# Holding back the fourth to seventh load at the start of a fused memory-attention and FFN kernel

## The chip, the cores and the metric

The kernel runs on one core of one Trainium2 chip. The metric is the device time of one execution in microseconds, lower is better; the time of the kernel before is the median of three runs.

## The reference

An attention over a small memory is followed by a bilinear feed-forward network without activation. Per batch (8) and head (8), with 576 positions, head width 64 and 32 memory slots:

```
a    = softmax(phi, over the 576 positions)          # [576, 32]
k_m  = a^T k ;  v_m = a^T v                          # [32, 64] each
attn = softmax(q k_m^T / 8, over the 32 slots)       # [576, 32]
x    = attn v_m                                      # heads side by side: [4608, 512]
out  = (((x w1) * (x w2)) w3) w_out                  # w1, w2: 512 x 1024, w3: 1024 x 1024, w_out: 1024 x 512
```

q, k, v and phi are float32; the four weights are float64 in memory, so w3 is 8 MB and each of the other three 4 MB.

## The kernel before, in words

**Algebra.** Because nothing stands between `w3` and `w_out`, the kernel forms their product W once (L386 to L403, `product` and `keep`), and it folds the attention's values into `w1` and `w2` per batch (`memory_weights`, L288). What is left per batch is `ab_unit` (the two products and their elementwise product, L437) and `out_part` (the product with W, L464). Both run as three matmuls each on values split into a high and a low part.

**Start.** The tasks of the list `tasks` (L321 to L325) are pieces of the weights: 18 of them go through five rotating buffers called `raw` (`BUFS = 5`, L328), the first four 512 KB each, the rest 1024 KB each. In order they are: `w3` and `w_out` alternately (rows 0 to 127, 128 to 255, then 256 rows at a time), the other column half of `w3`, then `w1` and `w2`. `fetch(i)` (L334) issues the load of task i; `convert(i)` (L350) turns its float64 words into float32 with two instructions of ScalarE (L378, L379) and three of VectorE (L377, L381, L382). Converting frees the buffer of task i, and `next_tile` (L407) then fetches task i + 5 into it. So before the loop over `START` (L415) five loads are issued at once, and the sixth follows the first conversion, the seventh the second, and so on. The first matmuls, `product(0, k)` at L392, need the converted `w3` and `w_out` rows of step k: W00 the first two tasks, W01 the next two, W02 and W03 the fifth and the sixth.

**Order.** All loads and stores of the kernel go through one queue, that of SyncE (SP). The orders of SP and of TensorE are as written in the program (lists `START`, `FIRST`, `SECOND`, `STEADY`, L22 to L37; L574). The orders of ScalarE and VectorE are laid out when the kernel is built, by simulated times. In `START`, C is `next_tile`, Wrk is `product(r, k)`, Krk is `keep`, N one step of `memory_weights`; phi0, kv0 and q0 are the loads of batch 0 (`load_phi` L121, `load_kv` L126, `load_q` L140); top, exp, norm, turn, mem, blocks, sc, se, sn, pr are the steps of the attention. The SP order at the start is: tasks 0 to 4, 5, 6, 7, 8, phi0, 9, 10, 11, kv0 (four transfers), 12, q0, 13 and on.

Of the kernel before, what the change touches and what calls it, by code (L numbers as in the profile page):

```python
# [8 lines left out]
F32 = mybir.dt.float32  # L9
# [31 lines left out]
def memory_attention__then__bilinear_ffn_kernel(  # L41
# [21 lines left out]
    nc = tc.nc  # L63
    P = 128
    B, NG, _, S = qT.shape
    D = 64
    M = 32
    NT = 2
# [8 lines left out]
    const = ctx.enter_context(tc.tile_pool(name="const", bufs=1))  # L77
# [40 lines left out]

    loaded = {}

    def load_phi(b):  # L121
        t = att.tile([P, NT, S], F32, name="ph", tag="ph")
        nc.sync.dma_start(out=t, in_=phiT[b].rearrange("t p s -> p t s"))
        loaded["ph", b] = t

    def load_kv(b):  # L126
        t = []
        for i in range(0, 4, 2):
            x = att.tile([P, 2, 8 * 2 * D], F32, name=f"kv{i}", tag=f"kv{i}")
            src = kv[b, i * P : (i + 2) * P].rearrange("(c p) h x -> p c (h x)", c=2)  # L130
            nc.sync.dma_start(out=x, in_=src)
            t += [x[:, j] for j in range(2)]

        x = att.tile([P, NG * 2 * D], F32, name="kv4", tag="kv4")
        for j in range(NT):
            src = kv[b, 4 * P :, j * NG : (j + 1) * NG].rearrange("s h x -> s (h x)")
            nc.sync.dma_start(out=x[j * D : (j + 1) * D], in_=src)
        loaded["kv", b] = [*t, x]

    def load_q(b):  # L140
        t = att.tile([P, NG, S], F32, name="q", tag="q")
        nc.sync.dma_start(out=t, in_=qT[b].rearrange("g p s -> p g s"))
        loaded["q", b] = t

    LOADS = {"phi": load_phi, "kv": load_kv, "q": load_q}

    def load(what, b):
# [178 lines left out]
    FIRST_LATE = 18  # L326
# [7 lines left out]
    def fetch(i):  # L334
        if i >= len(tasks):
            return
        kind, _, n, src = tasks[i]
        if i < FIRST_LATE:
            raw = init.tile([P, CW * 2], I32, name="raw", bufs=BUFS)
        else:  # L340

            name = ("kv0", "kv2", "q")[(i - FIRST_LATE) % 3]
            shape = [P, NG, S] if name == "q" else [P, 2, 8 * 2 * D]
            raw = att.tile(shape, F32, name=name, tag=name).bitcast(I32)
            raw = raw.rearrange("p a b -> p (a b)")
        words = n * src.shape[2] // 2
        raws[i] = raw[:, : 2 * words].rearrange("p (k x) -> p k x", k=n)
        nc.sync.dma_start(out=raws[i], in_=src)

# [57 lines left out]
    def next_tile():  # L407
        i = next(todo)
        convert(i)
        fetch(i + BUFS if i + BUFS < FIRST_LATE + 3 else i + 3 if i >= FIRST_LATE else len(tasks))  # L410

    with tc.tile_pool(name="init", bufs=1) as init:
        steps = [attention(b) for b in range(B)]
        m0 = memory_weights(0)
        for i in range(BUFS):  # L415
            fetch(i)
        for what in START:
            if what == "C":
                next_tile()
            elif what[0] == "W":  # L420
                product(int(what[1]), int(what[2]))
            elif what[0] == "K":
                keep(int(what[1]), int(what[2]))
            elif what == "N":
                m0.pop(0)()
            elif what[:-1] in LOADS:
                load(what, 0)
            else:
                steps[0][what]()
# [148 lines left out]
```

## Time and profile before

| | |
|---|---|
| median of three runs | 551.29 us (550.37 to 552.06) |
| the profiled execution | 550.54 us, of which the span from the first to the last instruction is 548.7 us |
| TensorE clock granted | 0.999 of the full one over the span |
| DMA, whole span | 64.05 MB, mean 117 GB/s |
| loads and stores | one queue, 24,944 packets |

The profile is of one execution. Times in its views count from the first instruction. PE is TensorE's matmuls, PEld its weight loads, DVE VectorE, ACT ScalarE, SP SyncE; SPq is an instruction with which SP issues a transfer. What stands behind an arrow in brackets ended the engine's idle time. The landing of a load is when its last byte is known to have arrived; the view of transfers gives the time from issue to landing.

### The profile page before, as it was taken

Reading aid. Unit: us, or ns where it says so; the run is one execution under the profiler, and the core shown is the slowest. Engines: PE = TensorE matmul, PEld = TensorE weight load, DVE = VectorE, ACT = ScalarE, POOL = GpSimd, SP = SyncE. Lnnn points to the kernel's source line nnn. Section 1 sums busy time; section 2 is a strip of 40 time slices with the busy share of each in tenths; the row PEclk is TensorE's granted clock in tenths of the full one; section 3 lists DMA queues with packets and bytes.
Section 4 is the critical chain, followed back from the end, with each engine's and each line's share of the span. In section 5 each row is a group of like instructions: output and inputs, shape, how many; then the busy total and the mean of one; then the engine's idle time right before and its main releaser. Section 6 shows DMA issues by size and latency. Waiting matters only on the chain.

```text
span 548.7 us, 9731 instructions
## 1 busy us (share of the span) xinstructions
PE 531.0 (97%) x4024; PEld 427.6 (78%) x4024; DVE 313.4 (57%) x600; ACT 249.9 (46%) x494; POOL 0.7 (0%) x6
## 2 busy tenths in 40 slices
PE   4899999999999999999999999999999999999997
PEld 1344357976998689968996899869986899689985
DVE  4877999557367715593458425673567045915400
ACT  5886966524554325452544335443544044514310
POOL 0000000000000000000000000000000000000000
PEclk9999999999999999999999999999999999999999
DMA  8999828036334510082007210351012100010011
GB/s 295 410 355 391 305 77 270 33 111 231 113 143 168 174 39 21 1 278 82 20 1 280 81 39 1 151 173 56 2 58 69 39 20 2 21 44 14 1 38 57
DMA packets 24987, 64.05 MB, mean 117 GB/s; under 512 B 1776, under 2 KB 2032, under 8 KB 24944
## 3 DMA queue, kind: packets, MB, share of 16 engines
q1 hardware_dynamic: 24944, 63.45, 32.6%
q8 instruction: 31, 0.51, 0.4%
q14 instruction: 12, 0.10, 0.1%
HBM read 54.00 MB, written 9.44 MB: 116 GB/s over the span
## 4 chain that ended last, share of the span: by engine, by line
PE 89%; DVE 7%; DMA 2%; issue 1%; ACT 1%; SPq 0%; DVEq 0%; ACTq 0%
PE o L472 37%; PE b L449 18%; PE a L449 18%; PE a L298 2%; PE a L392 2%; PE b L392 2%; DMA raw<-in_w3T 2%; DVE w L382 2%; PE o L199 2%; PE x L298 2%; PE x L184 1%; PE b L298 1%; PE x L199 1%; PE x L239 1%; DVE w L381 1%
## 5 line engine op out<-in xcount | busy, mean ns | idle before, releaser
L472 PE MATMUL o<-Wh,gh 128*128 128x512 f32 x288 | 115.4, 401 | 0.0
L472 PE MATMUL o<-Wl,gh 128*128 128x512 f32 x288 | 112.8, 391 | 0.0
L472 PE MATMUL o<-Wh,gl 128*128 128x512 f32 x288 | 112.5, 391 | 0.0
L460 DVE TENSOR_TENSOR gr<-b,a_sb 128x288 f32<-128x288 f32 x128 | 58.6, 458 | 85.9 <-PE b L449 82.0
L115 ACT CAST gh<-gr 128x288 fp32r<-128x288 f32 x128 | 55.4, 433 | 100.3 <-DVE gr L460 100.3
L116 DVE TENSOR_TENSOR gl<-gr,gh 128x288 fp32r<-128x288 f32 x128 | 58.6, 458 | 58.9 <-ACT gh L115 58.5
L449 PE MATMUL b<-ah,mh 128*128 128x288 f32 x256 | 76.0, 297 | 1.8 <-DVE gr L460 1.2
L449 PE MATMUL a<-ah,mh 128*128 128x288 f32 x256 | 77.2, 301 | 0.0
L449 PE MATMUL a<-al,mh 128*128 128x288 f32 x256 | 75.6, 295 | 0.1
L449 PE MATMUL b<-al,mh 128*128 128x288 f32 x256 | 75.5, 295 | 0.0
L449 PE MATMUL a<-ah,ml 128*128 128x288 f32 x256 | 75.3, 294 | 0.0
L449 PE MATMUL b<-ah,ml 128*128 128x288 f32 x256 | 75.3, 294 | 0.0
L472 PEld LDWEIGHTS o<-Wh,gh 128*128 128x128 f32 x288 | 54.1, 188 | 22.6 <-issue 11.9
L490 ACT COPY osb<-o 128x512 f32<-128x512 f32 x31 | 18.2, 586 | 100.1 <-PE o L472 87.4
L472 PEld LDWEIGHTS o<-Wl,gh 128*128 128x128 f32 x288 | 54.1, 188 | 12.4
L472 PEld LDWEIGHTS o<-Wh,gl 128*128 128x128 f32 x288 | 54.1, 188 | 10.9
L458 ACT COPY a_sb<-a 128x288 f32<-128x288 f32 x128 | 50.3, 395 | 3.5 <-PE a L449 3.1
L449 PEld LDWEIGHTS a<-ah,mh 128*128 128x128 f32 x256 | 48.0, 187 | 3.0 <-issue 1.0
L449 PEld LDWEIGHTS b<-ah,mh 128*128 128x128 f32 x256 | 48.0, 187 | 2.5 <-DVE gr L460 1.7
L449 PEld LDWEIGHTS a<-al,mh 128*128 128x128 f32 x256 | 48.1, 188 | 0.7 <-DVE al L116 0.3
L449 PEld LDWEIGHTS b<-ah,ml 128*128 128x128 f32 x256 | 48.2, 188 | 0.0
L449 PEld LDWEIGHTS a<-ah,ml 128*128 128x128 f32 x256 | 48.2, 188 | 0.0
(97 smaller groups left out, 650.8 us busy)
## 6 DMA issues: line engine op xcount, KB each, us to landing
kv<-in_kv SPq DMA_DIRECT2D x16, 1024.0 KB, 7.4
q<-in_qT SPq DMA_DIRECT2D x8, 1152.0 KB, 10.5
out<-osb SPq DMA_DIRECT2D x31, 256.0 KB, 2.0
raw<-in_w3T SPq DMA_DIRECT2D x7, 1024.0 KB, 11.8
ph<-in_phiT SPq DMA_DIRECT2D x8, 576.0 KB, 3.9
raw<-in_w SPq DMA_DIRECT2D x4, 1024.0 KB, 17.6
raw<-in_w_out SPq DMA_DIRECT2D x3, 1024.0 KB, 10.4
kv<-in_w SPq DMA_DIRECT2D x3, 1024.0 KB, 14.5
```

The costliest lines, as they stand in the source:

```text
L115: nc.scalar.copy(out=hi, in_=src)
L116: nc.vector.tensor_tensor(out=lo, in0=src, in1=hi.bitcast(F32), op=ALU.subtract)
L184: nc.tensor.transpose(ps[:, c, t], v["ph"][:, t, at : at + P], ident)
L199: nc.tensor.matmul(ps[t][h * M : (h + 1) * M, : 2 * D], lhsT=v["a"][:, i, t, h * M : (h + 1) * M], rhs=kvt[i][:, (4 * t + h) * 2 * D : (4 ...
L298: nc.tensor.matmul(ps[t][g * M : (g + 1) * M], lhsT=vm[b % 2][d, g], rhs=w12_sb[q][d, :, g], start=True, stop=True,)
L382: nc.vector.tensor_tensor(out=y, in0=y, in1=u, op=ALU.add)
L392: nc.tensor.matmul(pw[r][i], lhsT=x[:, i * P : (i + 1) * P], rhs=wos[k // half][:, k % half], start=k == 0, stop=k == NF - 1,)
L449: nc.tensor.matmul(p, lhsT=x[:, t, w, fc : fc + P], rhs=y[:, n, t * HALF : (t + 1) * HALF], start=i == 0, stop=i == len(todo) - 1,)
L458: nc.scalar.copy(out=a_sb, in_=ps[0])
L460: nc.vector.tensor_tensor(out=gr, in0=ps[1], in1=a_sb, op=ALU.mult)
L472: nc.tensor.matmul(v["p"], lhsT=x[f][:, at : at + P], rhs=y[f // half][:, f % half], start=f == 0 and k == 0, stop=f == NF - 1 and k == 2,)
L490: nc.scalar.copy(out=osb, in_=v["p"])
```

## The change

A one-row tile `gate` is added, and a helper `one_by_one`, called just ahead of the load of each `raw` tile and of batch 0's phi, kv and q. It counts the loads. Ahead of the load numbers 3, 4, 5 and 6 (counted from 0; the fourth to the seventh) it issues, in the same SP queue, a transfer of four bytes from the first element of an earlier load's tile into `gate`: number 3 behind number 0, 4 behind 1, 5 behind 3, 6 behind 4. Because that transfer reads what the earlier load writes, SP waits for that load's landing before it issues the four bytes; the load behind them is issued next and doesn't wait for the four bytes to land. Ahead of all other loads nothing is added.

```
+    BEHIND = {3: 0, 4: 1, 5: 3, 6: 4}
+    flights = []
+    gate = const.tile([1, 64], F32, name="gate")
+
+    def one_by_one(dst, words):
+        n = len(flights)
+        if n in BEHIND:
+            nc.sync.dma_start(out=gate[:, n : n + 1], in_=flights[BEHIND[n]][0])
+        flights.append([dst, words, False])
...
     def load_phi(b):
         t = att.tile([P, NT, S], F32, name="ph", tag="ph")
+        if b == 0:
+            one_by_one(t[:1, 0, :1], P * NT * S)
         nc.sync.dma_start(out=t, in_=phiT[b].rearrange("t p s -> p t s"))
...
         words = n * src.shape[2] // 2
+        if i < FIRST_LATE:
+            one_by_one(raw[:1, :1].bitcast(F32), P * 2 * words)
         raws[i] = raw[:, : 2 * words].rearrange("p (k x) -> p k x", k=n)
         nc.sync.dma_start(out=raws[i], in_=src)
```

The two calls left out, in `load_kv` and `load_q`, have the same form; none of the calls there or in `load_phi` issues anything, since those loads' numbers are not in `BEHIND`.

## Rows read from the trace of the kernel before

**Rows 1.** Stages of the span (view of windows): start and end, length, busy time and count of instructions of PE, PEld, DVE, ACT and POOL, granted clock, DMA share, GB/s.

```profile
0.00:20.00 20.00, 9.45 (x17) 4.04 (x18) 11.65 (x19) 13.11 (x15) 0.70 (x6) 1.00 0.90 332
20.00:49.00 29.00, 28.21 (x164) 13.36 (x162) 22.37 (x32) 20.62 (x25) 0.00 (x0) 1.00 1.03 379
49.00:87.00 38.00, 35.56 (x159) 18.20 (x158) 37.65 (x57) 29.62 (x34) 0.00 (x0) 1.00 0.59 214
87.00:548.70 461.70, 457.77 (x3687) 392.04 (x3687) 241.75 (x494) 186.56 (x421) 0.00 (x0) 1.00 0.24 83
```

**Rows 2.** The chain of waits that ended last, its start in order of time: start, length, what.

```profile
2.11 0.43 SPq L348
2.55 0.04 issue
2.59 10.64 DMA raw<-in_w3T
13.23 0.02 issue
13.26 1.17 ACT w L378
14.43 1.26 ACT u L379
15.69 0.02 issue
15.71 1.23 DVE w L382
...
18.30 1.24 DVE wo L382
19.54 0.04 issue
19.58 1.12 PE a L392 x2
...
40.58 0.86 PE b L392 x2
41.44 1.89 PE x L199 x64
```

**Rows 3.** Timeline of SP's issues: start, length of the issue, what.

```profile
0.73 0.39 SPq L348 DMA_DIRECT2D raw<-in_w3T  x1
1.18 0.42 SPq L348 DMA_DIRECT2D raw<-in_w_out  x1
1.64 0.43 SPq L348 DMA_DIRECT2D raw<-in_w3T  x1
2.11 0.43 SPq L348 DMA_DIRECT2D raw<-in_w_out  x1
2.59 0.47 SPq L348 DMA_DIRECT2D raw<-in_w3T  x1
5.36 0.37 SPq L348 DMA_DIRECT2D raw<-in_w_out  x1
7.36 0.37 SPq L348 DMA_DIRECT2D raw<-in_w3T  x1
10.68 0.37 SPq L348 DMA_DIRECT2D raw<-in_w_out  x1
12.08 0.37 SPq L348 DMA_DIRECT2D raw<-in_w3T  x1
12.50 0.46 SPq L123 DMA_DIRECT2D ph<-in_phiT  x1
...
85.82 0.89 SPq L131 DMA_DIRECT2D kv<-in_kv  x2
86.76 1.17 SPq L137 DMA_DIRECT2D kv<-in_kv  x2
87.97 0.59 SPq L142 DMA_DIRECT2D q<-in_qT  x1
```

**Rows 4.** View of transfers, asked for one issue at a time, for the first to the eighth load in that order, then the last of kv0's four (issued at 23.87 us): KB, and us from issue to landing.

```profile
raw<-in_w3T SPq DMA_DIRECT2D x1, 512.0 KB, 3.2
raw<-in_w_out SPq DMA_DIRECT2D x1, 512.0 KB, 4.8
raw<-in_w3T SPq DMA_DIRECT2D x1, 512.0 KB, 7.6
raw<-in_w_out SPq DMA_DIRECT2D x1, 512.0 KB, 8.6
raw<-in_w3T SPq DMA_DIRECT2D x1, 1024.0 KB, 10.6
raw<-in_w_out SPq DMA_DIRECT2D x1, 1024.0 KB, 10.4
raw<-in_w3T SPq DMA_DIRECT2D x1, 1024.0 KB, 11.0
raw<-in_w_out SPq DMA_DIRECT2D x1, 1024.0 KB, 10.2
...
kv<-in_kv SPq DMA_DIRECT2D x1, 128.0 KB, 16.6
```

**Rows 5.** Windows around the first loads, and around a later burst of issues (the last two rows); columns as in rows 1.

```profile
1.50:4.50 3.00, 0.00 (x0) 0.00 (x0) 0.46 (x1) 1.02 (x2) 0.00 (x0) 1.00 0.85 322
4.50:9.50 5.00, 1.38 (x2) 0.84 (x3) 2.83 (x6) 2.37 (x5) 0.00 (x0) 1.00 0.92 261
9.50:13.00 3.50, 3.50 (x6) 1.39 (x5) 2.75 (x6) 2.50 (x4) 0.00 (x0) 1.00 1.03 424
13.00:20.00 7.00, 4.56 (x11) 1.82 (x10) 5.61 (x7) 6.45 (x6) 0.00 (x0) 1.00 1.03 413
20.00:30.00 10.00, 10.00 (x25) 4.38 (x24) 9.03 (x14) 8.39 (x11) 0.00 (x0) 1.00 1.03 407
...
88.00:90.00 2.00, 2.00 (x24) 1.00 (x23) 1.84 (x7) 1.81 (x6) 0.00 (x0) 1.00 1.00 408
90.00:92.50 2.50, 2.50 (x21) 2.50 (x20) 2.47 (x5) 1.76 (x4) 0.00 (x0) 1.00 1.02 408
```

**Rows 6.** The shortest landings of the trace by median (page, DMA issues): stores of the result.

```profile
out<-osb SPq DMA_DIRECT2D x31, 256.0 KB, 2.0
```

More of the change, by code (lines that the diff above doesn't have):

```diff
@@ L130, in load_kv @@
             src = kv[b, i * P : (i + 2) * P].rearrange("(c p) h x -> p c (h x)", c=2)
+            if b == 0:
+                one_by_one(x[:1, 0, :1], P * 16 * 2 * D)
             nc.sync.dma_start(out=x, in_=src)
@@ L141, in load_q @@
         t = att.tile([P, NG, S], F32, name="q", tag="q")
+        if b == 0:
+            one_by_one(t[:1, 0, :1], P * NG * S)
         nc.sync.dma_start(out=t, in_=qT[b].rearrange("g p s -> p g s"))
```

## The prediction, made before the changed kernel ran

> **What bounds the kernel now.** I read the stages first [rows 1]. From 87 us to the end TensorE is busy 457.77 of 461.70 us at a granted clock of 1.00; the change touches nothing there, so that part only moves as a block. From 49 to 87 us VectorE is busy 37.65 of 38.00 us, again a block. From 20 to 49 us TensorE is busy 28.21 of 29.00 us. Only the first 20 us hold idle time: TensorE works 9.45 us of them. Next the chain of waits [rows 2]: it runs through SP's issues, then one load, the fifth (issued at 2.59 us, landed 10.64 us later at 13.23), then ScalarE and VectorE converting that load and the sixth, and reaches TensorE at 19.58 us, from where TensorE goes on to the attention step at 41.44 us. So what the change can be worth is how much earlier or later the fifth and sixth load land. Adding issue and landing time [rows 3, 4], the loads land at 3.9, 6.0, 9.2, 10.7, 13.2, 15.8, 18.4 and 20.9 us: in the order of issue, and from the fifth on one every 2.6 us, which is the queue at full rate, 407 to 424 GB/s [rows 5]. Between 4.5 and 9.5 us the rate was 261 GB/s although the DMA engines were busy for a 0.92 share [rows 5]: that slump is the one thing a different order of issue could cure.
>
> **The change part by part.**
>
> *The four small issues.* An issue takes SP 0.37 to 0.47 us [rows 3], so four take about 1.7 us. SP has nothing else to do at those times except the loads behind, so they count only through those.
>
> *The delays of issue.* The fourth load (2.11 us now) waits for the first landing: 3.9, plus 0.45 for the small issue, so about 4.4. The fifth (2.59) waits for the second: about 6.5. The sixth (5.36) waits for the fourth: about 11.2. The seventh (7.36) waits for the fifth: about 13.7. Queued behind it on SP are the eighth (10.68), the ninth (12.08) and phi (12.50), which go out at about 14.1, 14.6 and 15.1.
>
> *Does a landing move for it?* The first load took 3.2 us for 512 KB [rows 4]; at 413 GB/s its bytes take 524/413 = 1.27 us, so 1.95 us is what a load pays besides its bytes. From a landing to the landing that the released load could reach on an idle queue it is therefore 0.45 + 1.95 = 2.4 us plus its own bytes. What covers this are the loads still queued: the second and third behind the first, the third and fourth behind the second, the fifth behind the fourth, the sixth behind the fifth. Each time that is 1024 KB, 1049/413 = 2.54 us. The cover is enough by 0.14 us per gate, and by more in the slump. The eighth load must start to flow when the seventh's bytes end, just before 18.4 us; issued at 14.1, it has 1.95 us to spare twice over. I take 0.1 us for all four; without the cover each would cost up to 2.4 us.
>
> *The small transfers themselves* are not in the trace of before. A lower end is nothing. An upper end is the shortest landing, 2.0 us [rows 6], if the queue stood still for each: four of them, 8 us. A gain has no mechanism here. The release doesn't wait for the four bytes to land; they also read the buffers that the sixth, seventh, ninth and tenth load overwrite, but lie in the queue behind loads that land before those overwrites are due. I take 0, by the issues of rows 3 that follow one another without a stop.
>
> *The slump.* Upper end of the gain: if everything behind the first landing flowed at 413 GB/s, the second to fifth load (2560 KB, 2621/413 = 6.35 us) would be in at 3.9 + 6.35 = 10.3 instead of 13.2, 2.9 us earlier. By the bytes alone, 261 GB/s over 5.0 us, 1305 KB, lose 5.0 - 1305/413 = 1.84 us. Lower end: nothing, or less than nothing if fewer queued loads ran slower still. I take no change, because the rate doesn't follow the number of loads queued: from 20 to 30 us five or more were under way (landing times of 10 us and more at one landing per 2.6 us) at 407 GB/s [rows 4, 5], and after a burst of five issues within 3 us at 86 to 88 us the first megabytes came at 408 GB/s [rows 3, 5]. Moreover the slump begins while the second and third load flow, and these are issued as before.
>
> The Trainium skill, page "DMA: Bandwidth & Descriptors", section on latency and other measured facts, says that an access to HBM takes ten times longer under high load than on average; read so, fewer queued loads would shorten the early ones, and the sum would lie nearer the upper end of the gain. The 407 GB/s with more loads queued speak against it here.
>
> *What moves behind.* Had the fifth and sixth load landed earlier, conversion would follow: ScalarE starts on the fifth at 13.26, 0.03 us after its landing [rows 2]. TensorE's block from 19.58 would move with it as far as kv0 lets it: its last part lands at 23.87 + 16.6 = 40.5, 0.9 us before its use at 41.44 [rows 2, 4]; beyond 0.9 us the gain needs kv0 earlier too, which it would be, being behind in the same queue.
>
> *The orders of ScalarE and VectorE* are laid out at build by simulated times, and four more transfers could swap two steps; one conversion instruction is 1.23 us [rows 2]. I take 0.
>
> **Sum:** 0.1 us on 550.54 us of the profiled execution (span 548.7, 1.8 around it): 550.6. The median of the runs stands 0.75 above that execution, 551.29, so I predict 551.3 on the scale of the medians.
>
> **The rivals.**
>
> *A, my forecast: the gates are passed under cover and the landings stay.* This is also the case in which the change doesn't do what it says: four loads are issued later and none arrives at another time, since the queue serves them in order. 551.3, from 551.0 to 552.0.
>
> *B: the slump goes, wholly or in good part.* For it: the slump falls in the only stretch that follows a burst of five issues from an empty queue, and the low rate at a 0.92 share says that each packet was slow, not that packets were lacking. Against it: the rates of rows 5 with as many loads queued. The gain lies between 1.5 (half of 2.9) and 2.9 us; midway between the two full cures, 1.84 and 2.9, it is 2.4: 548.9, from 548.4 to 549.8. VectorE's block from 49 us would pass it on if its loads are earlier too.
>
> *C, slower: the queue runs dry behind a gate.* The margin of 0.14 us per gate is thin. If a four-byte transfer holds up the loads behind it, or a released load starts later than 1.95 us says, each gate exposes up to 2.0 us [rows 6]. The sixth and seventh load are most at risk, with a single load as cover: one exposure gives 553.3, both 555.3. It decides from 1.75 us in all (0.44 per gate). For it: no row shows such a transfer in a stream of loads. Against it: SP's issues in rows 3 overlap the flow of earlier loads everywhere without a gap in the rate.
> The Trainium skill says the same as a rule: page "DMA: Bandwidth & Descriptors", rules for kernel authors, asks to issue transfers early so that the fixed cost overlaps, which its section on the anatomy of a DMA puts at about 2.0 us. By that rule, with nothing covered, four gates would give an estimate of 8 us. The 1.95 us of the first load agrees with the size; that it is exposed no row shows.
>
> **How the numbers follow.** About 0.3%, 1.65 us, is what a measurement of this kernel can tell from no change: below 549.6 is faster, above 552.9 slower. A gets 0.45, B 0.37, C 0.18. A lies within the bound but for 0.01 on either side. Of B, 0.35 is beyond it and 0.02, a half cure or a cure that VectorE's block swallows, within. Of C, 0.17 is beyond. So faster 0.36, same 0.46, slower 0.18. The range runs from 548.2 (all of B, with 0.2 us for the spread of runs) to 552.6 (A with the spread of runs of 0.77 above the median, and the mildest of C); it leaves out about 0.15 of C and some 0.03 of B. Since A and B together hold most of the chance and differ in sign, A's own range is 551.0 to 552.0.
>
> **What would show it.** In the profile of the changed kernel SP's issues of the fourth to seventh load should stand near 4.4, 6.5, 11.2 and 13.7 us, each behind a small issue of about 0.4 us. If A holds, ScalarE starts on the fifth load (the first 128x1024 conversion) at 13.1 to 13.6 us, TensorE's long run starts at 19.4 to 20.0, and the rate from 4.5 to 9.5 us stays below 300 GB/s. B would show that rate near 400 and the run at 16.6 to 18. C would show a rate below 400 between 10 and 20 us, landings more than 2.6 us apart behind a gate, and the run from 21 us on. The forecast is wrong if the run on TensorE starts over 1.6 us away from 19.58, or if the stretch from 20 to 87 us changes in length by more than 1 us, which would point to the orders of ScalarE and VectorE.

## The result: 4 us slower, and the profile after

The changed kernel takes 555.04 us (median of 13 runs, 551.56 to 557.23); the kernel before, on the same chip, 550.70 (13 runs). The ratio is 1.0072, with an interval of 1.0058 to 1.0086: 3.2 to 4.7 us slower. The profiled execution took 553.82 us with a span of 552.0, 3.3 over that of before.

First the timeline of the changed kernel, SP's issues and two of the instructions that wait (start, length, what). The four-byte transfers are issued at L128, and the lines named here stand higher than before: the loads are L366, the conversion L395 to L400, the first products L410 (18 higher each), the attention step L215 (16 higher).

```profile
1.64 0.43 SPq L366 DMA_DIRECT2D raw<-in_w3T  x1
4.05 0.73 SPq L128 DMA_DIRECT2D gate<-raw  x1
4.83 0.34 SPq L366 DMA_DIRECT2D raw<-in_w_out  x1
5.29 0.61 SPq L128 DMA_DIRECT2D gate<-raw  x1
5.94 0.38 SPq L366 DMA_DIRECT2D raw<-in_w3T  x1
9.80 0.59 SPq L128 DMA_DIRECT2D gate<-raw  x1
10.52 0.37 SPq L366 DMA_DIRECT2D raw<-in_w_out  x1
12.32 0.59 SPq L128 DMA_DIRECT2D gate<-raw  x1
13.02 0.37 SPq L366 DMA_DIRECT2D raw<-in_w3T  x1
...
17.27 1.15 ACT L396 ACTIVATE wo<-raw 128x1024 f32<-128x1024 f32 x1 [2.53 <-DMA raw<-in_w_out]
...
20.98 1.17 PE L410 MATMUL a<-wo,w 128*128 128x512 f32 x2 [4.19 <-DVE wo L400]
```

The gates do what they say: the fourth to seventh load go out at 4.83, 5.94, 10.52 and 13.02 us instead of 2.11, 2.59, 5.36 and 7.36 [rows 3]. Next, from the view of transfers for one issue at a time, the landings of the third to the seventh load (KB, us from issue):

```profile
raw<-in_w3T SPq DMA_DIRECT2D x1, 512.0 KB, 6.0
raw<-in_w_out SPq DMA_DIRECT2D x1, 512.0 KB, 5.0
raw<-in_w3T SPq DMA_DIRECT2D x1, 1024.0 KB, 6.4
raw<-in_w_out SPq DMA_DIRECT2D x1, 1024.0 KB, 6.7
raw<-in_w3T SPq DMA_DIRECT2D x1, 1024.0 KB, 8.0
```

With the issue times these are 7.6, 9.8, 12.3, 17.2 and 21.0 us, against 9.2, 10.7, 13.2, 15.8 and 18.4 before [rows 3, 4]. The third to fifth load come 0.9 to 1.6 us earlier, the sixth 1.4 later, 4.9 us behind the fifth instead of 2.6. The windows show why (columns as in rows 1): first the stages, then the first loads, then the stretch around TensorE's restart.

```profile
0.00:20.00 20.00, 9.10 (x16) 3.75 (x16) 10.54 (x18) 11.36 (x13) 0.70 (x6) 1.00 0.83 284
20.00:49.00 29.00, 27.24 (x142) 13.21 (x143) 21.92 (x31) 21.42 (x26) 0.00 (x0) 0.94 1.03 386
49.00:87.00 38.00, 35.86 (x161) 16.65 (x160) 36.54 (x55) 28.07 (x32) 0.00 (x0) 1.00 0.61 224
...
1.50:4.50 3.00, 0.00 (x0) 0.00 (x0) 0.44 (x1) 0.96 (x2) 0.00 (x0) 1.00 0.93 330
4.50:9.50 5.00, 1.82 (x2) 0.83 (x3) 3.85 (x9) 3.49 (x6) 0.00 (x0) 1.00 0.88 289
9.50:11.00 1.50, 1.50 (x3) 0.67 (x2) 1.13 (x3) 1.19 (x2) 0.00 (x0) 1.00 1.01 407
11.00:12.50 1.50, 1.50 (x4) 0.70 (x3) 0.86 (x2) 0.33 (x2) 0.00 (x0) 1.00 0.70 120
13.00:20.00 7.00, 3.78 (x9) 1.33 (x7) 3.76 (x6) 4.13 (x4) 0.00 (x0) 1.00 0.96 338
...
16.80:20.90 4.10, 0.00 (x0) 0.00 (x0) 2.65 (x3) 2.39 (x2) 0.00 (x0) 1.00 1.01 363
20.98:21.92 0.94, 0.94 (x2) 0.48 (x3) 0.78 (x1) 0.85 (x1) 0.00 (x0) 1.00 1.03 423
21.93:25.33 3.40, 3.40 (x5) 1.33 (x4) 2.50 (x4) 3.21 (x4) 0.00 (x0) 0.50 1.03 412
25.34:36.00 10.66, 10.66 (x26) 4.75 (x25) 9.25 (x14) 9.30 (x11) 0.00 (x0) 1.00 1.03 409
```

From 11.0 to 12.5 us the queue ran dry: 120 GB/s, where the kernel before had 424 from 9.5 to 13 us [rows 5]. From 13 to 20 us the rate is still lower than before (338 against 413). And a second thing, which the profile of the kernel before doesn't show at this place: after TensorE had nothing to do from 16.8 to 20.9 us, its granted clock was 0.50 from 21.93 to 25.33, the 1.2 GHz level. The chain that ended last shows both with their price (start, length, what):

```profile
10.52 6.73 DMA raw<-in_w_out
17.25 0.02 issue
17.27 1.15 ACT wo L396
...
20.98 1.17 PE a L410 x2
22.15 1.71 PE b L410 x2
23.85 1.66 PE a L410 x2
25.52 0.86 PE b L410 x2
...
44.53 1.89 PE x L215 x64
```

TensorE's long run starts at 20.98 instead of 19.58 [rows 2], 1.40 us later. Two of its pairs of matmuls take 1.71 and 1.66 us instead of 0.86: another 1.65. The attention step then starts at 44.53 instead of 41.44, 3.1 us later, and that is nearly all of the 3.3 us by which the spans differ.

The path is the one that the prediction followed. In the profiles of both kernels and of all ten experiments, TensorE's long run starts 3.7 to 3.9 us behind the landing of the sixth load.

### The profile page after: what moved, and what is told of

It reads as the page before. It is cut to its first block, busy times and chain, and to the rows that moved or that the text cites. A ratio compares the mean times of both kernels' runs of the same rounds, so it can differ in the third digit from the quotient of the medians.

```text
span 552.0 us, 9734 instructions
## 1 busy us (share of the span) xinstructions
PE 532.9 (97%) x4024; PEld 428.2 (78%) x4024; DVE 313.8 (57%) x600; ACT 249.3 (45%) x494; POOL 0.7 (0%) x6
## 4 chain that ended last, share of the span: by engine, by line
PE 88%; DVE 6%; DMA 3%; issue 1%; ACT 1%; SPq 0%; ACTq 0%; DVEq 0%
PE o L490 36%; PE b L467 18%; PE a L467 18%; PE a L410 2%; PE b L410 2%; PE a L314 2%; DMA raw<-in_w_out 2%; PE o L215 2%; PE x L314 2%; DVE w L400 1%; PE x L200 1%; PE b L314 1%; PE x L215 1%; PE x L255 1%; DVE w L399 1%
## 6 DMA issues: line engine op xcount, KB each, us to landing
raw<-in_w SPq DMA_DIRECT2D x4, 1024.0 KB, 16.4
raw<-in_w_out SPq DMA_DIRECT2D x3, 1024.0 KB, 10.7
```

## The experiments

All times are medians with the ratio to the kernel before run beside them on the same chip, and its interval. Each run also has a mean clock of TensorE; a run below 0.9985 has had a stretch at half clock somewhere. The kernel before has it too, in 12 of 28, 9 of 35 and 6 of 21 runs beside these experiments, though its profile shows half clock only in the last 0.8 us. The changed kernel had it in 12 of 13. A mean clock doesn't tell where the stretch was.

**Two early gates alone.**

```
-    BEHIND = {3: 0, 4: 1, 5: 3, 6: 4}
+    BEHIND = {3: 0, 4: 1}
```

> Only the fourth and fifth load are gated (behind the first and second); the sixth and seventh go out as soon as their buffers are free. Theory (the two late gates run the queue dry at 11 to 12.5 us and TensorE's wait of 4.2 us then costs it its clock, while the two early gates shorten the slump): the fifth load lands near 12.3 us, the sixth near 14.9, TensorE's long run starts near 18.6 instead of 20.98, the clock stays 1.00, the time is 1 us below the kernel before, 549.7. Rival (any gate breaks the flow, early ones too): the run starts after 20 us and the time is 552 or more.

551.87 us against 551.83, ratio 0.9998 (0.9975 to 1.0020). The rate from 11.0 to 12.5 us, in the view of windows:

```profile
11.00:12.50 1.50, 1.50 (x5) 0.62 (x4) 0.60 (x1) 0.00 (x0) 0.00 (x0) 1.00 0.96 371
```

No dry stretch, and on the median no harm, so by its time the rival falls. But the gain that the theory gave them isn't there either: the fifth load landed at 13.9 and the sixth at 16.5, though the third was in at 7.3, 2 us earlier than before. And the profiled execution, at 552.97 us one of the 5 of 12 with a mean clock below 0.9985, shows a sign of the rival: TensorE's run starts after 20 us, and from 21.5 to 24.9 us the clock is at half, where the theory had 1.00.

```profile
20.29 1.13 PE L410 MATMUL a<-wo,w 128*128 128x512 f32 x2 [3.78 <-DVE wo L400]
```

**Two late gates alone.**

```
-    BEHIND = {3: 0, 4: 1, 5: 3, 6: 4}
+    BEHIND = {5: 3, 6: 4}
```

> Only the sixth and seventh load are gated (behind the fourth and fifth); the first five go out together as before. Theory (the late gates do the whole harm): the slump and the fifth landing at 13.2 us are as in the kernel before, a stretch without data follows, the sixth load lands near 18, TensorE waits over 4 us, the time is 555 us or a little more, about 1 us above the change as given. Rival (the harm is in the early gates): TensorE's run starts near 19.6 and the time is that of the kernel before, 550.7.

552.96 us, ratio 1.0027 (1.0011 to 1.0043). Slower, but only by 1.5 us, so neither forecast came true, and the sixth load landed at 16.4, not 18: the queue also ran low (202 GB/s from 11.0 to 12.5), yet the released load needed 4.8 us from issue to landing, against 6.7 in the change. The late gates cost more where the early ones stand in front of them.

**Four small transfers, behind loads that land earlier.**

```
-    BEHIND = {3: 0, 4: 1, 5: 3, 6: 4}
+    BEHIND = {3: 0, 4: 0, 5: 1, 6: 2}
```

> The same four transfers of four bytes, but behind loads that land earlier: the fourth and fifth load behind the first, the sixth behind the second, the seventh behind the third. Theory (the small transfers cost nothing, the waits do): no stretch without data after 10 us, TensorE's run starts at 18.5 to 19.8, the clock stays 1.00, 549.7 to 551 us. Rival (each four-byte transfer holds up the queue): landings behind each of them come more than 2.6 us apart, the run starts after 20.5, 553 us or more.

552.0 us against 551.83, ratio 1.0004 (0.9984 to 1.0023); 385 GB/s from 11.0 to 12.5. Four transfers of four bytes in the queue cost nothing that can be measured (the interval is 1 us either way). TensorE's run started at 19.28, as the theory had it; the clock did not stay at 1.00 but was at half from 19.6 to 23.0 us, behind a wait of only 1.97 us:

```profile
19.28 1.83 PE L410 MATMUL a<-wo,w 128*128 128x512 f32 x2 [1.97 <-DVE wo L400]
```

**Filling TensorE's wait.** The change, and a step F behind W01 in `START`:

```
+            elif what == "F":
+                x = psum_pair()
+                for i in range(4):
+                    nc.tensor.matmul(x[:, i % 2], lhsT=wos[0][:, 0, :P], rhs=wos[0][:, 0], start=True, stop=True)
```

> The change as given, with four more matmuls (128x512, on data that is already there, into a bank that nobody reads) between the second product and the wait for the sixth load, 3.4 us of work that ends before that wait does. Theory (part of the harm is that TensorE, after 4.2 us without work, runs at half clock for 3.4 us): the clock stays 1.00, the time falls by about 1.7 us to 553 us, and the runs spread less. Rival (the late landing alone is the harm and the clock follows nothing that TensorE did): 555 us with the clock at half for some us, as without the four.

555.53 us, ratio 1.0076 (1.0047 to 1.0106): no fall. The clock was 1.00 from 22 to 30 us, as the theory wants, but this kernel isn't a clean test. The added matmuls changed the simulated times, and with them the orders of ScalarE and VectorE; TensorE's run started at 22.14 instead of 20.98, and the profile has its half clock at another place:

```profile
85.57:88.97 3.40, 3.40 (x14) 3.40 (x15) 3.40 (x5) 1.25 (x3) 0.00 (x0) 0.50 0.40 147
```

So the next ones use fewer and shorter instructions, which leave those orders as they were.

**The late gates one load earlier.**

```
-    BEHIND = {3: 0, 4: 1, 5: 3, 6: 4}
+    BEHIND = {3: 0, 4: 1, 5: 2, 6: 3}
```

> All four gates, but the sixth load behind the third and the seventh behind the fourth, one load earlier than in the change. Theory (the queue runs dry because, when the fourth load has landed, half of the fifth's bytes, the only cover, have flowed already): no slice without data at 11 to 12.5 us, the rate from 9.5 to 13 us above 380 GB/s instead of 253, the sixth load lands near 15.3 instead of 17.25, and the time is that of the two early gates alone, 551 to 552 us. Rival (a landing gate on the sixth and seventh load costs its wait whatever load it looks at, for SP is held and the eighth and ninth stand behind): 554 us or more.

552.19 us, ratio 1.0020 (1.0000 to 1.0041), beside the early gates' 0.9998. The sixth load went out at 8.16 and landed 7.6 us later, at 15.8 instead of 17.2:

```profile
9.50:11.00 1.50, 1.50 (x3) 0.63 (x2) 0.90 (x3) 1.33 (x2) 0.00 (x0) 1.00 1.10 363
11.00:12.50 1.50, 1.50 (x3) 0.68 (x2) 0.69 (x1) 0.02 (x1) 0.00 (x0) 1.00 0.96 268
12.50:14.00 1.50, 1.50 (x4) 0.58 (x3) 0.72 (x1) 0.72 (x1) 0.00 (x0) 1.00 0.99 393
```

The queue no longer stands still (a DMA share of 0.96, not 0.70), TensorE's run starts at 19.64, and most of the loss is gone. Half of its runs, 6 of 12, still have the half clock, with a median of 553.5 against 550.5 in the others. The rate, 324 GB/s from 9.5 to 13 us, is below the 380 expected. With the same number of gates, the same SP instructions and the same loads behind them, the landing that is waited for decides.

**TensorE's wait shortened in the kernel before, in the change, and in the two early gates.** The same edit in all three, in `START` and its loop:

```
-C C C C phi0 W00 top W01 C C C exp
+C C C C phi0 W00 top W01 F C C C exp
...
+            elif what == "F":
+                x = psum_pair()
+                for i in range(8):
+                    nc.tensor.transpose(x[:, i % 2, :P], ident, ident)
```

> The kernel before with eight 128x128 transposes of the identity, 0.9 us on TensorE, between the second product and the wait for the sixth load, into a bank that nobody reads; the orders of ScalarE and VectorE stay as they were. TensorE's idle time ahead of its long run shrinks from 2.4 to 1.5 us. Theory (the idle time decides how often an execution gets a stretch at half clock, which costs 1.7 us): fewer than 3 of 12 runs show it, against 12 of 28 of the kernel before, and the median falls to 550.4. Rival (the stretch at half clock comes by chance or from another engine): the share and the median stay.

550.81 us against 550.72, ratio 0.9998 (0.9986 to 1.0010). The transposes end at 17.65, the wait is 2.06 us:

```profile
16.61 1.04 PE L423 MATMUL x<-ident 128*128 128x128 f32 x8
19.71 0.70 PE L392 MATMUL a<-wo,w 128*128 128x512 f32 x1 [2.06 <-DVE wo L382]
```

One run of 11 has a stretch at half clock, against 9 of 35 without the transposes. The median doesn't fall, for two reasons: on this chip most runs of the kernel before had none anyway, and the runs without it take 550.79 with the transposes and 550.53 without. The share fell as told, though 1 of 11 and 9 of 35 can't be told apart from chance; the median was told wrong.

> The change as given with the same eight transposes; TensorE's idle time shrinks from 4.2 to about 3.3 us. Theory: still over the 2.4 us of the kernel before, so nearly all runs still have a stretch at half clock, but fewer with two; 554 us. Rival as in the run beside it: nothing moves, 555.

553.80 us, ratio 1.0039 (1.0022 to 1.0057). The wait is still 3.4 us:

```profile
16.07 1.04 PE L441 MATMUL x<-ident 128*128 128x128 f32 x8
20.55 1.02 PE L410 MATMUL a<-wo,w 128*128 128x512 f32 x1 [3.44 <-DVE wo L400]
```

8 of 12 runs have the half clock, none with a mean clock below 0.9945, where the change had 5 of 13 such. The four runs without it have a median of 552.09, the eight with it 554.37: 2.3 us between them.

> The two early gates alone with the eight transposes. Theory: the early gates bring the third load 1.7 us earlier but not the fifth and sixth, so their own gain is none, and the transposes keep the clock in most runs: 550.5, beside 551.9 without them. Rival: as without the transposes, 551.9.

551.17 us, ratio 1.0006 (0.9987 to 1.0024); the wait is 1.15 us in the profile, and 2 of 12 runs have the half clock, against 5 of 12 without the transposes. Theory and rival lie too close for this to part them. None of these versions beats the kernel before.

**One late gate at a time, with the early ones.**

```
-    BEHIND = {3: 0, 4: 1, 5: 3, 6: 4}
+    BEHIND = {3: 0, 4: 1, 5: 3}        # the first of the two
+    BEHIND = {3: 0, 4: 1, 6: 4}        # the second
```

> The change without the gate of the seventh load; the sixth still waits for the fourth's landing. Theory (a gate whose only cover is one load that has half flowed empties the queue): the stretch without data at 11 to 12.5 us stays, the sixth lands at 16.5 to 17.3, TensorE waits 3.5 us or more, and the median is 553.5 to 555. Rival (it takes both late gates, the second one on the seventh load doing the larger part): sixth landing near 15.5, 552.

555.42 us, ratio 1.0068 (1.0042 to 1.0095): the whole loss, with one late gate. The sixth load, out at 10.51, landed 7.4 us later at 17.9, later than expected. TensorE waited 4.41 us. The clock fell within that wait, at 19.6, and rose at 26.4: 6.8 us at half, of which TensorE worked 4.74, against 3.40 in the profile of the change.

```profile
11.00:12.50 1.50, 1.50 (x3) 0.68 (x2) 0.87 (x2) 0.32 (x2) 0.00 (x0) 1.00 0.64 98
...
19.00:21.60 2.60, 0.00 (x0) 0.00 (x0) 1.92 (x3) 2.41 (x4) 0.00 (x0) 0.61 1.02 416
21.66:26.40 4.74, 4.74 (x6) 2.16 (x7) 4.46 (x6) 4.43 (x5) 0.00 (x0) 0.50 1.03 406
```

> The change without the gate of the sixth load; the seventh still waits for the fifth's landing. Theory: the queue runs dry once, later, near 14 us; the sixth load, on which TensorE's long run waits, is in front of that and lands near 16, so TensorE waits no longer than with the two early gates, 551.5 to 552.5; the seventh and the ones behind come 1 to 2 us later and are waited for by ScalarE, not by TensorE. Rival (any late gate does the harm): 553.5 or more.

553.47 us, ratio 1.0018 (1.0001 to 1.0036): the median lies at the rival's 553.5, the ratio at the theory's 551.5 to 552.5, so this run decides nothing about the time. The queue runs dry later, as expected, with the sixth load in front of the gap (landed at 15.6), and TensorE waits 2.29 us:

```profile
14.00:16.00 2.00, 2.00 (x6) 0.93 (x5) 1.12 (x2) 1.93 (x3) 0.00 (x0) 1.00 0.66 152
```

The median falls beside a gap in its runs, five of them at 551.0 to 552.1 and six at 553.5 to 553.7; a ratio of 1.0018 is 1 us. Two of the six slower ones have a mean clock of 0.999 or more, so the half clock alone doesn't make the gap.

## Why the prediction was wrong

**The cover behind the sixth load's gate is the step that failed.** The prediction counted the cover behind each landing as 1024 KB, 2.54 us, and found it enough by 0.14 us. But here the load that stood behind another in the queue flowed in part before that one's landing was known. By 9.8 us, when the fourth load had landed, 330 GB/s over 3.0 us, 289 over 5.0 and 407 over 0.3 had moved 990 + 1445 + 122 = 2557 kB. The first five loads together are 3072 KB, 3146 kB. So only 589 kB of the fifth were left, 1.45 us at 407 GB/s. The small issue took 0.59 us and the load was issued 0.72 us behind the landing, not 0.45; by the prediction's own term, 1.95 us that a load pays besides its bytes, its bytes could flow 1.2 us after the queue was empty, at about 11.2. The price of an exposure, up to 2.0 us, had the right size: the sixth load landed 4.9 us behind the fifth instead of 2.6, which is 2.3 us, and net of the 0.9 us by which the fifth came earlier, 1.4. The run with the gates of the fourth, fifth and sixth load shows that one late gate suffices; the one with the late gates a load earlier, that the landing chosen is what matters.

So rival C, with a chance of 0.18, had the right outcome, a queue run dry behind the sixth load's gate, but not the main reason, a cover smaller than counted. Of its own two reasons the first is out, since the small transfers cost nothing that can be measured. The second, a released load that starts later than 1.95 us says, may have a part: the sixth load took 6.7 us, 4.2 more than its bytes at 413 GB/s. The range, which ended at 552.6, left it out. That C's price for two exposures, 555.3, lies next to the measured 555.04 is luck: one late gate alone brings 555.42, and half of the loss in the profile comes from the clock, which C doesn't have.

**The clock was not in the sum at all.** The prediction read 1.00 everywhere and took TensorE's wait of 2.4 us as given. In the profile the stretch at half clock behind the wait of 4.19 us cost 1.65 us more, and the change nearly always has one. By the wait in the profile, the shares are 1 of 11 runs at 2.06 us, 9 of 35 at 2.4, 8 of 12 at 3.4, 12 of 13 at 4.2 and 10 of 11 at 4.4. So the longest waits bring the half clock in most runs. The transposes leave the rest of the program as it is, and in all three pairs the share is lower with them, but none of the pairs alone is clear of chance. The wait isn't the whole rule either: the early gates alone had 5 of 12 at 3.78 us. Of single profiles, those with waits of 1.97, 2.29, 2.31 and 2.39 us have the half clock at TensorE's restart, and those with 2.06, 2.44 and 2.58 us don't. What decides there is open. The Trainium skill, page "TensorE: Matmul & The Clock Gate", section on why this matters for kernels, says that idle gaps between bursts of matmuls bring the half rate back; the 12 of 13 runs at 4.2 us agree, and at 2.4 us the case is already undecided from run to run. An execution with the half clock is slower than one without by 2.3 us in the change with transposes and by 1.8 (552.32 - 550.53) in the kernel before.

**The slump.** "No change" was wrong too. With fewer loads queued the rate from 4.5 to 9.5 us was 288 to 314 GB/s in every profile with early gates and 243 to 261 in those without, and the third load landed at 7.1 to 7.6 us instead of 9.2 to 9.3. So a small part of rival B came true, far from the 400 GB/s that it asked for. It led nowhere: in the two profiles with the early gates alone the fifth load landed at 13.9 and 13.2 us and the sixth at 16.5 and 15.7, no earlier than before, and the time stayed. Why, these runs don't show.

**What held.** The stages behind the attention step moved as a block: from it to the end of the span are 507.5 us, 507.3 before. The issue times were within 0.7 us of those told. The four-byte transfers cost nothing that can be measured. The orders of ScalarE and VectorE are the same in both kernels. Three slips in the working changed nothing: 3.2 less 1.27 us is 1.93, not 1.95; 551.29 and 0.1 make 551.4; and landing times of 10 us at one landing per 2.6 make four loads under way, though the issue times of the trace do give five at 20 us.

**What stays open.** A late landing of 1.3 us (552.09 in the runs of the change with transposes that kept the clock, less the 550.79 of the kernel before with them) and a half clock in nearly every run, some 2 us, make 3.3 us, the difference of the two profiles. The medians differ by 4.3. The other executions of the change were not traced. Five of the 13 have a mean clock of 0.992 to 0.994 and lie at 555.0 to 557.2; the profile of the change without its last gate, with a clock of 0.992, has 6.8 us at half instead of 3.4, so a stretch of that length is the likely cause of part of the rest. The runs with a mean clock of 0.996 or 0.997 still lie at 553.8 to 555.4. A sixth load that lands later still, as the 17.9 us of that profile, would do it, but this wasn't shown. Nor is it shown why the released load takes 6.7 to 7.5 us behind early gates and 4.8 without them. With the late gates alone the working above would give an exposure of 1.8 us (2.72 MB moved at the fourth landing, issue 0.88 us behind it), and the sixth load landed 3.2 us behind the fifth, 0.6 more than before.

## What to carry to other kernels

A load that is released by another's landing is covered only by what has not yet flowed at that moment: count the bytes moved until then, not the bytes queued behind. So gate at least one load further back than the sum of sizes asks for, which here removed most of the loss and brought no gain, and only if the rate of the ungated queue shows a loss that waiting can mend. When a change lengthens a wait of TensorE, price the clock behind it as well: in the profile here it cost 1.65 us beside the later start's 1.40.

## What the runs showed of the hardware that was not expected

After the queue had run dry, the rate stayed low for several us in the change even though several loads were queued again: 338 GB/s from 13 to 20 us, against 413 before, and 370 with the sixth load's gate as the only late one. With the late gates alone it was back at 410 GB/s from 14 to 16 us, so this doesn't follow every dry stretch. The start of every one of these kernels is slow too, 243 to 314 GB/s from 4.5 to 9.5 us with or without gates. The slump of the kernel before may thus belong in the main to the start from an empty queue rather than to the burst of issues; the late gates made a second one. Against that speaks the burst at 86 us of the kernel before, which ran at 408 GB/s from 88 us on [rows 5]. This wasn't settled.
